# Spreading the first FFN matmul over the attention stages, with its result kept in HBM

## The chip, the cores and the metric

The kernel runs on one core of a Trainium2 chip. The metric is the device time of one execution in microseconds; the time shown is the median of three runs. Engines are named as in the profile: PE is the matmul engine (PEld its weight loads), DVE the vector engine, ACT the scalar engine, POOL GpSimd, and SP the queue that issues every DMA of this kernel. Matmul results go to PSUM, of which the kernel uses eight banks of 128x512 floats.

## The reference

The input x has 2048 rows of 512. Two branches read its layer norm, and the result joins them:

```
xn  = layernorm(x)                                   # [2048, 512]
q, k, v = split(xn @ wqkv)                           # 32 heads of 16
phi(t)  = [softmax(t @ w_phi), softmax(-t @ w_phi)]  # per head, 16 -> 32
kv  = sum over s of phi(k)^T v;   z = sum over s of phi(k)
o   = phi(q) kv / (phi(q) z + 1e-6)
s   = o @ wo
h   = xn @ w1 + b1                                   # [2048, 1792]
g   = silu(mish(h) @ w2)
out = x + s * g
```

Everything is float32. The kernel gets this precision out of the fast matmul format by splitting each operand into a high part hi (rounded) and a low part lo = operand - hi; each product is three matmuls (lo·hi, hi·lo, hi·hi), which is what `mm3` issues.

## The kernel before

The rows are worked in 16 tiles of 128 (t = 0 to 15), in 8 pairs u, and for the FFN in 4 groups g of 512 rows. The 1792 hidden columns make 14 chunks of 128, that is 7 blocks of 256 per group.

The kernel doesn't issue its instructions where they are written. Each call on PE, V (DVE), G (POOL), A (ACT) or Q (SP) is recorded as an `Op` with what it reads and writes. A planner (`Program.simulate`) then plays the program through with a cost for each instruction (`cost`), picks for each engine the ready operation with the earliest due time `late`, and `issue` emits the instructions in the order of the planned starts. The order on PE is not free: it is the order in which the parts are written in the string `ORDER`. An operation recorded by `either` or `copy` may go to one of two engines, which the planner chooses. On the chip each engine then works strictly in the emitted order, and SP's queue too.

The parts in `ORDER`:

- `wk`, `wq`: load the k and q weights and fold w_phi into them (four fp32 matmul groups each), split; `wv`, `wo`: load and split.
- `N t` (`norm`): load x, statistics on DVE, the power -0.5 on POOL (rs), scale, transpose on PE (pt), split into xT, and store xT to HBM (scr) for the FFN.
- `K t` (`k_proj`): 12 matmuls of 128x512, then the double softmax: copy from PSUM (ACT), max and min over 16 (DVE, km), two subtractions (POOL, into ke), exponential (ACT), sums and reciprocal (DVE, ks and kr), scaling (ke), split into kh (ACT) and kl. `Q t` is the same without the split. `V t`: 12 matmuls and a split into vh, vl. `A t` (`kv_acc`): 24 matmuls with 128 columns that add phi(k)^T v into two PSUM banks; v carries a column of ones, which gives z.
- `z` (`sums`): takes kv and z out of PSUM after the last A.
- `D t` (`den`): product with z (ez) and its sums (tz), reciprocal, scaling of phi(q). `T`: transposes of phi(q) (pp) and their split (ph). `U`: 12 matmuls with 256 columns (pn), split into oh, ol. `O t`: 12 matmuls (pw) with wo, stored to HBM (so).
- `P b`, `R b`: load and split block b of w1, w2. `L g`: load group g's xT from scr (tiles fh, fl of the pool; PE's output banks bear the name fh as well).
- `F` (`ffn1`): first FFN matmul of a block, 24 matmuls of 128x512 in two banks, each followed by Mish on ACT, into a tile r that stays in SBUF. `G` (`ffn2`): split of r into ah, al, and 24 matmuls that add into the group's four y banks; the last two blocks of the last group are done together. `E g` (`final`): silu through Tanh, the product, the residual, the store.

Before the change q's projection of a tile stands between the k and v work of the tiles, and of the 28 F blocks six stand ahead of the first G; the other 22 alternate with the G blocks. All SBUF tiles of 4 KB a partition come from one pool of 43 slots, those of 2 KB from one of 11.

Of the kernel before, what the change touches and what calls it, by code (L numbers as in the profile page):

```python
# [28 lines left out]
PEN, HOLD, MARGIN = 8000, 300, 1000  # L29
BACK, COLD = 1500, 0  # L30

SLOTS, S2 = 43, 11
SLACK, AHEAD, LAT = 15000, 40000, 150
ORDER = """
wk K0 wv N2 K1 wq N3 V0 Q0 K2 N4 A0 V1 Q1 K3 N5 A1 V2 Q2 N6 K4 A2 V3 wo K5 Q3 N7 A3 V4 Q4 K6 N8 A4 V5 Q5 K7 N9
A5 V6 Q6 K8 N10 A6 V7 Q7 K9 N11 A7 V8 Q8 K10 N12 A8 V9 Q9 K11 N13 A9 V10 Q10 K12 N14 A10 V11 N15 Q11 b1 P0 K13
A11 V12 L0 P1 Q12 K14 K15 A12 V13 Q13 P2 A13 V14 Q14 A14 V15 Q15 A15 z F0 F1 D0 D1 T0 T1 F2 D2 U0 D3 T2 U1 D4
T3 D5 D6 T4 O1 U2 O0 T5 U3 D7 U4 D9 T6 O3 D8 T7 U5 P3 O2 F3 U6 T8 T9 D11 O4 U7 O5 D10 T10 T11 U8 P4 D12 U9 D13
F4 O7 T12 T13 O8 D14 D15 O6 U10 U11 O9 T14 T15 U12 O11 U13 U14 U15 O13 O10 O12 P5 F5 O15 R0 O14 G0 R1 G1 R2 G2
R3 G3 R4 P6 F6 G4 L1 R5 F7 G5 R6 F8 G6 E0 F9 G7 F10 G8 F11 G9 F12 G10 F13 L2 G11 F14 G12 F15 G13 E1 F16 G14  # L40
F17 G15 F18 G16 F19 G17 F20 G18 L3 F21 G19 F22 G20 E2 F23 G21 F24 G22 F25 G23 F26 F27 G24 G25 G26 E3
"""
# [3 lines left out]
class Op:  # L46
    __slots__ = ("impl", "reads", "writes", "at", "idx", "succ", "ndep", "late", "new", "ready", "start", "eng", "sets", "slack", "open", "soon", "pos", "deps")


class Program:  # L50


    def __init__(self, nc):
        self.eng = {"PE": nc.tensor, "V": nc.vector, "G": nc.gpsimd, "A": nc.scalar, "Q": nc.sync}
        self.ops, self.tag, self.cap, self.pe = [], {}, {}, []
        self.group, self.slack = None, SLACK

# [27 lines left out]
    def add(self, impl, reads, writes, sets=()):  # L85
        o = Op()
        o.impl, o.reads, o.writes, o.idx, o.sets, o.slack = impl, reads, writes, len(self.ops), sets, self.slack
        o.pos = len(self.pe)
        if "PE" in impl:
            self.pe.append(o)  # L90
        self.ops.append(o)
# [64 lines left out]
    def simulate(self, at):  # L156
# [20 lines left out]
        aset = 0  # L177
        dma = 0
        events = [(500, 2, -1)]
# [22 lines left out]
        def go(o, e):  # L202
            nonlocal aset, dma
            dur, calls = o.impl[e]
# [13 lines left out]
            if e == "Q":  # L218
                nb = calls[0][1][0].free_size() * 128 * 4
                dma = max(dma, now + 1100) + nb / 360  # L220
                end = dma + 1000
                heapq.heappush(events, (dma - BACK, 2, -1))
# [93 lines left out]
def block_kernel(ctx: ExitStack, tc: tile.TileContext, x, wqkT, wv, phi, wo, w1, b1, w2, out):  # L316
# [8 lines left out]
    pools = {}  # L325
    for tag, n in (("slot", SLOTS), ("s2", S2), ("sm", 13), ("rq", NT), ("st", 2 * NT)):
        pools[tag] = ctx.enter_context(tc.tile_pool(name=tag, bufs=n))
        prog.cap[tag] = n
# [13 lines left out]
    def slot(shape, name, dtype=F32):  # L342
        return alloc("slot", shape, name, dtype)
# [90 lines left out]

    def load_pairs(src, name):
        r = []
        for i in range(2):
            t = slot([P, 2, D], f"{name}r{i}")
            Q.dma_start(t, src[2 * i * P:2 * (i + 1) * P, :].rearrange("(c p) k -> p c k", p=P))
            hi, lo = split_raw(t, f"{name}{i}")  # L440
            r += [(hi[:, j, :], lo[:, j, :]) for j in range(2)]
        return r

# [63 lines left out]

    def k_proj(t, between=None):
        r = sm([P, 2 * H], f"k{t}r")
        ek[t] = softmax(proj(t, w["k"], "k", between), f"k{t}", r)  # L510
        e = ek[t].rearrange("p h s d -> p (h s d)")
        scale(ek[t], r)
        ek[t] = [slot([P, 2 * D], f"k{n}{t}", F32R) for n in "hl"]
        split(e, *ek[t], either)
# [36 lines left out]

    def tr_q(t):
        u, j = divmod(t, 2)
        if j == 0:
            phT[u] = [[slot([P, 4, 2 * P], f"ph{u}{i}{v}", F32R) for v in range(2)] for i in range(2)]
        e = eq.pop(t).rearrange("p h s d -> p (h s d)")
        cs = slice(j * P, (j + 1) * P)
        for i in range(2):
            pp = bank([P, 4, P], f"pp{t}_{i}")
# [54 lines left out]

    def ffn1(B):
        g, b = divmod(B, NB)
        wh, wl = w1_[b]
        q = slot([P, 2, D], f"r{B}")
        for j2 in range(2):
            f = 2 * b + j2  # L620
            ph = bank([P, D], f"fh{B}_{j2}")
            fs = slice(j2 * P, (j2 + 1) * P)
            with one():
                for k in range(KC):
                    i, kk = divmod(k, 2)
                    mm3(ph, (wh[:, k, fs], wl[:, k, fs]), (fx[g][2 * i][:, kk, :], fx[g][2 * i + 1][:, kk, :]),
                        k == 0, k == KC - 1)
# [49 lines left out]

    def first_k():
        w["k"] = fold(wkT, "wk", 0) + fold(wkT, "wk", 1, lambda: norm(0))

    def weights_v():
        w["v"] = load_pairs(wv, "wv")

    def weights_q():
        t = load_wT(0, "wq", 0) + load_wT(0, "wq", 1)
        w["q"] = fold(t, "wq", 0) + fold(t, "wq", 1)

    def weights_o():
        w["o"] = load_pairs(wo, "wo")

# [26 lines left out]

    def first_proj():
        k_proj(0, lambda: norm(1))

    def att_num(t):
        num(t // 2, t % 2)
# [38 lines left out]
```

## Time and profile before

| | |
|---|---|
| median of three runs | 614.62 us (613.53 to 615.33) |
| the profiled execution's own time | 612.32 us |
| its span, first to last instruction | 610.6 us |
| mean granted TensorE clock | 0.976 |
| busy: PE, DVE, ACT, POOL | 575.0, 357.4, 231.8, 220.7 us |
| DMA | 49.8 MB, mean 82 GB/s |

The page's rows are read so: a busy time is followed by the share of the span and the number of instructions; the slices divide the span into 40 parts of 15.3 us, and a digit is the busy share in tenths. PE's end times are modelled and its matmuls overlap, so PE's busy time is an upper bound of its work. Since everything goes through one helper line, instructions are told apart by their tiles: `al<-r,ah` is the instruction that writes a tile al from r and ah.

### The profile page before, as it was taken

What the parts mean: (1) busy time and instruction counts of PE and PEld (TensorE: products, weight loads), DVE (VectorE), ACT (ScalarE), POOL (GpSimd) and SP (SyncE); (2) the same over time, 40 slices, a digit from 0 to 9 for tenths busy, and PEclk for the clock granted to TensorE, in tenths of its full rate; (3) what the DMA queues carried; (4) which work ended last, traced back from release to release, by engine and by line L of the source; (5) the groups of instructions that cost most, each with busy time, mean ns of one, the idle gap of its engine ahead of it and who ended that gap; (6) DMA issues with size and microseconds to landing.
All of it is one profiled execution on the core that took longest, in us unless ns stands there. A gap on an engine that the chain in (4) does not pass through costs nothing.

```text
span 610.6 us, 7532 instructions
## 1 busy us (share of the span) xinstructions
PE 575.0 (94%) x2998; PEld 484.0 (79%) x2998; DVE 357.4 (59%) x496; ACT 231.8 (38%) x318; POOL 220.7 (36%) x156
## 2 busy tenths in 40 slices
PE   6989999799969978799999999999999999999996
PEld 5868788688758767688888888888888888888885
DVE  6999978888698899999583210801108011081115
ACT  3634444544545442243474122622126221262221
POOL 2787778667666867453131100300003000030000
PEclk9999999989989997799999999999999999999999
DMA  8632212213610002010255700243002430023001
GB/s 283 236 104 79 77 53 74 65 36 101 197 48 0 1 1 70 22 58 27 100 178 185 263 15 0 86 142 119 1 0 89 137 119 0 1 88 137 0 1 69
DMA packets 42211, 49.81 MB, mean 82 GB/s; under 512 B 4160, under 2 KB 27456, under 8 KB 42176
## 3 DMA queue, kind: packets, MB, share of 16 engines
q1 hardware_dynamic: 42176, 49.33, 24.9%
q8 instruction: 23, 0.38, 0.2%
q14 instruction: 12, 0.10, 0.1%
HBM read 32.55 MB, written 16.78 MB: 81 GB/s over the span
## 4 chain that ended last, share of the span: by engine, by line
PE 58%; DVE 21%; POOL 13%; issue 3%; ACT 2%; DMA 1%; SPq 1%; POOLq 0%; DVEq 0%
PE y L300 25%; PE fh L300 21%; PE pw L300 5%; DVE tz L300 3%; PE pn L300 2%; DVE den L300 2%; DVE ph L300 1%; DMA wvr<-wv 1%; DVE x L300 1%; POOL kl L300 1%; PE v L300 1%; PE pp L300 1%; PE kv L300 1%; PE q L300 1%; POOL k2e L300 1%
## 5 line engine op out<-in xcount | busy, mean ns | idle before, releaser
L300 DVE TENSOR_TENSOR al<-r,ah 128x1024 fp32r<-128x1024 f32 x21 | 25.7, 1224 | 141.8 <-ACT ah L300 141.7
L300 ACT ACTIVATE r<-fh,b1t 128x512 f32<-128x512 f32 x56 | 38.1, 689 | 165.3 <-PE fh L300 165.3
L300 POOL TENSOR_TENSOR al<-r,ah 128x1024 fp32r<-128x1024 f32 x7 | 17.0, 2426 | 211.1 <-ACT ah L300 211.1
L300 PE MATMUL k<-wkh,xT 128*128 128x512 f32 x128 | 42.5, 393 | 0.7 <-DVE xT L300 0.7
L300 PE MATMUL q<-wqh,xT 128*128 128x512 f32 x128 | 42.1, 390 | 0.0
L300 PE MATMUL kv<-kh,vl 128*65 128x128 f32 x128 | 26.7, 240 | 12.3 <-DVE vl L300 11.6
L300 PEld LDWEIGHTS kv<-kh,vl 128*65 128x65 f32 x128 | 18.9, 147 | 14.6 <-DVE vl L300 14.4
L300 PE MATMUL pn<-ph,kvh 128*128 128x256 f32 x128 | 24.8, 293 | 5.8 <-DVE ph L300 5.8
L300 ACT ACTIVATE ah<-r 128x1024 fp32r<-128x1024 f32 x28 | 29.6, 1059 | 0.7
L300 PEld LDWEIGHTS k<-wkh,xT 128*128 128x128 f32 x128 | 24.0, 188 | 5.8 <-DVE xT L300 0.9
L300 PEld LDWEIGHTS q<-wqh,xT 128*128 128x128 f32 x128 | 24.0, 188 | 5.0
L300 PE MATMUL kv<-kl,vh 128*65 128x128 f32 x128 | 26.0, 235 | 0.7 <-DVE kl L300 0.7
L300 PE MATMUL kv<-kh,vh 128*65 128x128 f32 x128 | 25.9, 234 | 0.0
L300 PEld LDWEIGHTS pn<-ph,kvh 128*128 128x128 f32 x128 | 20.7, 199 | 6.5 <-DVE ph L300 6.3
L300 PE MATMUL v<-wv0h,xT 128*128 128x512 f32 x64 | 25.3, 437 | 0.0
L300 PE MATMUL k<-wkl,xT 128*128 128x512 f32 x64 | 24.9, 390 | 0.0
L300 PE MATMUL q<-wql,xT 128*128 128x512 f32 x64 | 24.9, 389 | 0.0
L300 PE MATMUL v<-wv1h,xT 128*128 128x512 f32 x64 | 22.7, 395 | 0.0
L300 DVE TENSOR_TENSOR ph<-pp,ph 128x512 fp32r<-128x512 f32 x32 | 20.6, 679 | 3.4 <-ACT ph L300 3.4
L300 DVE TENSOR_TENSOR sr<-yc,sr 128x512 f32<-128x512 f32 x12 | 20.4, 1699 | 0.5
L300 DVE COPY yc<-y 128x512 f32<-128x512 f32 x6 | 4.1, 685 | 27.6 <-PE y L300 27.6
L300 PEld LDWEIGHTS kv<-kl,vh 128*65 128x65 f32 x128 | 18.9, 148 | 1.3 <-DVE kl L300 0.9
(573 smaller groups left out, 1814.3 us busy)
## 6 DMA issues: line engine op xcount, KB each, us to landing
scr<-xT SPq DMA_DIRECT2D x16, 512.0 KB, 3.8
x<-x SPq DMA_DIRECT2D x16, 256.0 KB, 4.0
fh<-scr SPq DMA_DIRECT2D x8, 512.0 KB, 4.9
fl<-scr SPq DMA_DIRECT2D x8, 512.0 KB, 5.3
so<-so SPq DMA_DIRECT2D x16, 256.0 KB, 2.2
sr<-so SPq DMA_DIRECT2D x15, 256.0 KB, 5.2
xx<-x SPq DMA_DIRECT2D x15, 256.0 KB, 4.6
out<-xx SPq DMA_DIRECT2D x15, 256.0 KB, 2.0
```

The source lines that it names most:

```text
L300: getattr(e, m)(*a, **k)
```

## The change

F is cut in 56 pieces: one output chunk of 128 columns for a group of 512 rows, 12 matmuls of 128x512. Its bank is copied to a tile h by ACT or DVE, without bias or Mish, and stored to an HBM tile hd. G loads the two halves of its block from hd into r, applies Mish in place on ACT, and goes on as before. `ORDER` places 55 of the 56 pieces ahead of the first G, among K, V, A and Q, D, T, U, O; 15 of the 16 O tiles stand ahead of the first G as well, where before all 16 did. Loading w1 (`P`) and the groups (`L`) moves forward with the pieces. Most Q parts stand after the last A (seven tiles ahead of it, nine behind), and q reads its x from scr again instead of keeping xT. The halves of wk, wv, wq and wo are parts of their own, and T and U are cut by halves of the heads instead of tiles.

The planner changes in three ways. It keeps a time `port` until which the pair of VectorE and GpSimd is taken: an operation that `locks` names (any on G; on V those with two SBUF operands beside the output, or a wide tensor_scalar or copy, none reading PSUM) starts its duration only from then. DMA is planned with 250 instead of 360 bytes per ns. A PE operation no longer depends on an earlier PE operation, since PE works in order anyway.

```diff
-BACK, COLD = 1500, 0
+BACK, COLD, DRATE = 1500, 0, 250
...
+            if "PE" in o.impl:
+                dep = {d for d in dep if "PE" not in ops[d].impl}
...
+            if e in o.lock:
+                dur += max(0, port - now)
+                port = now + dur
...
-                dma = max(dma, now + 1100) + nb / 360
+                dma = max(dma, now + 1100) + nb / DRATE
...
+def locks(e, m, a):
+
+    if e == "G":
+        return True
+    aps = [v for v in a if isinstance(v, bass.AP)]
+    if e != "V" or any(v.space == "PSUM" for v in aps):
+        return False
+    return aps[0].free_size() > 1 if m in ("tensor_scalar", "tensor_copy") else len(aps) > 2
...
     def q_proj(t):
+        xT[t] = slot([P, 2, KC, P], f"xq{t}", F32R)
+        Q.dma_start(f32(xT[t]), scr[t // 4][:, :, :, t % 4, :])
...
-    def ffn1(B):
-        g, b = divmod(B, NB)
+    def ffn1(n):
+        g, f = divmod(n, FC)
+        b, j2 = divmod(f, 2)
         wh, wl = w1_[b]
...
-            A.activation(q[:, j2, :], ph, AF.Mish, bias=b1t[:, f:f + 1])
-        acts[B] = q
+        h = s2(f"h{n}")
+        copy(h, ph)
+        Q.dma_start(hd[g * NB + b][:, j2, :], h)
...
     def ffn2(B):
...
-            q = acts.pop(b)
...
+            q = slot([P, 2, D], f"r{b}")
+            Q.dma_start(q, hd[b])
+            for j2 in range(2):
+                f = 2 * (b % NB) + j2
+                A.activation(q[:, j2, :], q[:, j2, :], AF.Mish, bias=b1t[:, f:f + 1])
+            ah, al = split_raw(q, f"a{b}")
```

Of `ORDER`, the first lines stand so before and after:

```diff
-wk K0 wv N2 K1 wq N3 V0 Q0 K2 N4 A0 V1 Q1 K3 N5 A1 V2 Q2 N6 K4 A2 V3 wo K5 Q3 N7 A3 V4 Q4 K6 N8 A4 V5 Q5 K7 N9
+N0 N1 wv0 wk0 wk1 K1 N2 K0 wv1 V0 N4 N5 P0 N3 K3 A0 V1 K2 P2 L0 A1 V2 N6 K4 K5 P1 F2 F0 A2 V3 K6 P5 N12 A3 V4 wq0 N8
+N9 F3 P6 P3 P4 A4 V5 N7 F10 wq1 F12 N10 K7 F1 A5 V6 F6 K8 A6 V7 L1 N11 F4 F8 K10 F18 F19 F5 F14 A7 F13 V8 K9 F15 F16
```

PE in the first stage, around the projection k of tile 5 (names are tile, number, then the buffer's number). Before, q of tile 3 follows it:

```order
L300 MATMUL k5_266<-wkl1_136,xT5_235 128x512
L300 MATMUL k5_266<-wkh1_135,xT5_235 128x512
L300 MATMUL q3_274<-wqh0_181,xT3_193 128x512
L300 MATMUL q3_274<-wql0_182,xT3_193 128x512
L300 MATMUL q3_274<-wqh0_181,xT3_193 128x512 x2
```

After, the first FFN piece (chunk 2 of group 0) stands there, ahead of the kv sums of tile 2:

```order
L307 MATMUL k5_241<-wkl1_151,xT5_190 128x512
L307 MATMUL k5_241<-wkh1_150,xT5_190 128x512
L307 MATMUL fh2_252<-fh00_221,w11l_250 128x512
L307 MATMUL fh2_252<-fl00_222,w11h_249 128x512
L307 MATMUL fh2_252<-fh00_221,w11h_249 128x512
```

The piece needs tiles 0 to 3 normalised, stored and loaded again as a group (fh00, fl00), and w1's block 1 split (w11h, w11l). On SP's queue the same stretch before holds loads of x and stores of xT only:

```order
L300 DMA scr1_107<-xT4_214 1024x1x128
L300 DMA x9_321<-x 128x512
L300 DMA scr1_107<-xT5_235 1024x1x128
L300 DMA x10_342<-x 128x512
L300 DMA scr1_107<-xT6_248 1024x1x128
L300 DMA x11_363<-x 128x512
```

After, group 0, w1's blocks and the first pieces' stores stand in it:

```order
L307 DMA fh00_221<-scr0_106 128x1024
L307 DMA fl00_222<-scr0_106 128x1024
L307 DMA fh01_223<-scr0_106 128x1024
L307 DMA fl01_224<-scr0_106 128x1024
L307 DMA x9_287<-x 128x512
L307 DMA wqT00_276<-wqkT 128x4x256
L307 DMA x7_305<-x 128x512
L307 DMA w1r5_266<-w1 128x4x256
L307 DMA scr1_107<-xT6_230 1024x1x128
L307 DMA hd01_251<-h2_253 128x512
```

The loads of x for tile 8 and on, and of w1's next blocks, have moved behind the group's loads, and a store of h may stand ahead of a load. The third place is ACT in the second FFN stage. Before, it takes Mish of the blocks from PE's banks (fh):

```order
L300 ACTIVATE r12_811<-fh12_0_812,b1t_83 128x512
L300 ACTIVATE r12_811<-fh12_1_813,b1t_83 128x512
L300 ACTIVATE ah12_828<-r12_811 128x1024
L300 ACTIVATE r13_816<-fh13_0_817,b1t_83 128x512
L300 ACTIVATE r13_816<-fh13_1_818,b1t_83 128x512
L300 ACTIVATE ah13_833<-r13_816 128x1024
```

After, at the start of that stage, Mish reads the tile r that a DMA has brought back, between the last attention tiles (oh) and w2's splits:

```order
L307 ACT_TABLE_LOAD
L307 ACTIVATE r0_885<-r0_885,b1t_83 128x512 x2
L307 ACTIVATE a0h_886<-r0_885 128x1024
L307 ACTIVATE oh7_863<-pn7_0_865 128x512
L307 ACTIVATE r7_898<-r7_898,b1t_83 128x512 x2
L307 ACTIVATE oh7_863<-pn7_1_869 128x512
L307 ACTIVATE a7h_899<-r7_898 128x1024
```

Mish no longer waits for PE there, but for the load of r.

More of the change, by code (lines that the diff above doesn't have):

```diff
@@ L34 @@
 ORDER = """
-wk K0 wv N2 K1 wq N3 V0 Q0 K2 N4 A0 V1 Q1 K3 N5 A1 V2 Q2 N6 K4 A2 V3 wo K5 Q3 N7 A3 V4 Q4 K6 N8 A4 V5 Q5 K7 N9
[L36 to L41, printed above, removed]
+N0 N1 wv0 wk0 wk1 K1 N2 K0 wv1 V0 N4 N5 P0 N3 K3 A0 V1 K2 P2 L0 A1 V2 N6 K4 K5 P1 F2 F0 A2 V3 K6 P5 N12 A3 V4 wq0 N8
+N9 F3 P6 P3 P4 A4 V5 N7 F10 wq1 F12 N10 K7 F1 A5 V6 F6 K8 A6 V7 L1 N11 F4 F8 K10 F18 F19 F5 F14 A7 F13 V8 K9 F15 F16
+N13 A8 V9 F24 F11 F25 A9 V10 Q9 K11 F22 A10 V11 L2 F30 K12 F7 N14 F9 N15 K13 A11 V12 F20 Q4 K15 K14 Q0 A12 F21 V13 Q1
+A13 V14 F17 Q2 Q6 b1 A14 V15 Q5 A15 F23 z Q3 D0 F26 F27 D1 Q8 F28 F34 L3 T1 D3 T0 F32 D2 Q7 F31 Q12 F29 U0 U1 wo0 wo1
+T3 D6 F35 T2 F38 U2 U3 F36 F39 D5 F33 O0 D4 O1 F37 D7 D8 F42 F46 F43 F44 F40 Q10 F41 T6 T5 T4 Q11 U4 U5 T7 D9 T8 T9
+D12 Q13 Q14 D14 U8 U9 F50 U6 D11 U7 O2 F48 F49 F45 O3 F51 R2 O5 Q15 D10 T11 O8 D15 F54 F52 D13 T10 T12 O7 U10 O6 T13
+U11 R6 O9 F47 T15 T14 U12 U13 R0 O10 U14 R4 U15 O4 F53 O11 R3 O15 O13 O12 G0 R1 R5 G7 G8 G1 G2 G3 G4 G9 G10 G11 G5 G6
+O14 G12 E0 G13 E1 G14 G15 F55 G16 G17 G18 G19 G20 E2 G21 G22 G23 G24 G25 G26 E3
 """
@@ L46 @@
 class Op:
-    __slots__ = ("impl", "reads", "writes", "at", "idx", "succ", "ndep", "late", "new", "ready", "start", "eng", "sets", "slack", "open", "soon", "pos", "deps")
+    __slots__ = ("impl", "reads", "writes", "at", "idx", "succ", "ndep", "late", "new", "ready", "start", "eng", "sets", "slack", "open", "soon", "pos", "deps", "lock", "part")
 class Program:
@@ L55, in __init__ @@
         self.ops, self.tag, self.cap, self.pe = [], {}, {}, []
-        self.group, self.slack = None, SLACK
+        self.group, self.slack, self.part = None, SLACK, None
     @staticmethod
@@ L87, in add @@
         o.impl, o.reads, o.writes, o.idx, o.sets, o.slack = impl, reads, writes, len(self.ops), sets, self.slack
-        o.pos = len(self.pe)
+        o.pos, o.part = len(self.pe), self.part
+        o.lock = {e for e, (_, calls) in impl.items() if any(locks(e, m, a) for m, a, k in calls)}
         if "PE" in impl:
@@ L177, in simulate @@
         aset = 0
-        dma = 0
+        dma = port = 0
         events = [(500, 2, -1)]
@@ L202, in go @@
         def go(o, e):
-            nonlocal aset, dma
+            nonlocal aset, dma, port
             dur, calls = o.impl[e]
@@ L325, in block_kernel @@
     pools = {}
-    for tag, n in (("slot", SLOTS), ("s2", S2), ("sm", 13), ("rq", NT), ("st", 2 * NT)):
+    for tag, n in (("slot", SLOTS), ("s2", S2), ("sm", 13), ("rq", 5), ("st", 2 * NT)):
         pools[tag] = ctx.enter_context(tc.tile_pool(name=tag, bufs=n))
@@ L414, in load_wT, with fold @@
         return ts
-    def fold(wT, name, i, between=None):
+    def fold(wT, name, i):
         hi = slot([P, 2, D], f"{name}h{i}", F32R)
@@ L424, in fold @@
             split(ps, hi[:, j, :], lo[:, j, :])
-            if between and j == 0:
-                between()
         return [(hi[:, j, :], lo[:, j, :]) for j in range(2)]
@@ L433, in split_raw, with load_pair @@
         return hi, lo
[L435 to L442, printed above, removed]
+    def load_pair(src, name, i):
+        t = slot([P, 2, D], f"{name}r{i}")
+        Q.dma_start(t, src[2 * i * P:2 * (i + 1) * P, :].rearrange("(c p) k -> p c k", p=P))
+        hi, lo = split_raw(t, f"{name}{i}")
+        return [(hi[:, j, :], lo[:, j, :]) for j in range(2)]
     scr = [dram.tile([P, 2, KC, 4, P], F32, name=f"scr{g}") for g in range(NG)]
@@ L470, in norm, with proj @@
         Q.dma_start(scr[t // 4][:, :, :, t % 4, :], f32(w))
-    def proj(t, w, name, between=None):
+    def proj(t, w, name):
         ps = bank([P, D], f"{name}{t}")
@@ L477, in proj @@
                     mm3(ps, (xT[t][:, 0, k, :], xT[t][:, 1, k, :]), w[k], k == 0, k == KC - 1)
-            if between and i == 0:
-                between()
         return ps
@@ L506, in block_kernel, with k_proj @@
     ek, eq, rq, phT, oT = {}, {}, {}, {}, {}
-    def k_proj(t, between=None):
+    def k_proj(t):
         r = sm([P, 2 * H], f"k{t}r")
[L510 to L514, printed above, removed]
+        e = softmax(proj(t, w["k"], "k"), f"k{t}", r)
+        scale(e, r)
+        ek[t] = split_raw(e.rearrange("p h s d -> p (h s d)"), f"k{t}")
     def q_proj(t):
+        xT[t] = slot([P, 2, KC, P], f"xq{t}", F32R)
+        Q.dma_start(f32(xT[t]), scr[t // 4][:, :, :, t % 4, :])
         rq[t] = alloc("rq", [P, 2 * H], f"q{t}r")
@@ L550, in den, with tr_q @@
         scale(eq[t], r)
[L552 to L559, printed above, removed]
+    def tr_q(n):
+        u, i = divmod(n, 2)
+        phT[n] = [slot([P, 4, 2 * P], f"ph{u}{i}{v}", F32R) for v in range(2)]
+        for j in range(2):
+            e = eq[2 * u + j].rearrange("p h s d -> p (h s d)")
+            cs = slice(j * P, (j + 1) * P)
+            pp = bank([P, 4, P], f"pp{2 * u + j}_{i}")
             with one():
@@ L562, in tr_q, with num @@
                     PE.transpose(pp[:, c, :], e[:, (4 * i + c) * P:(4 * i + c + 1) * P], ident)
-            split(pp, phT[u][i][0][:, :, cs], phT[u][i][1][:, :, cs])
-    def num(u, i):
-        ph = phT[u][i]
+            split(pp, phT[n][0][:, :, cs], phT[n][1][:, :, cs])
+    def num(n):
+        u, i = divmod(n, 2)
+        ph = phT.pop(n)
         if i == 0:
@@ L604, in prep2 @@
         w2_[b] = split_raw(t, f"w2{b}")
+    hd = {}
     def load_g(g):
@@ L613, in load_g @@
                 fx[g].append(t)
-    def ffn1(B):
-        g, b = divmod(B, NB)
+    def ffn1(n):
+        g, f = divmod(n, FC)
+        b, j2 = divmod(f, 2)
         wh, wl = w1_[b]
[L618 to L627, printed above, removed]
-            A.activation(q[:, j2, :], ph, AF.Mish, bias=b1t[:, f:f + 1])
-        acts[B] = q
+        if j2 == 0:
+            hd[g * NB + b] = dram.tile([P, 2, D], F32, name=f"hd{g}{b}")
+        ph = bank([P, D], f"fh{n}")
+        fs = slice(j2 * P, (j2 + 1) * P)
+        with one():
+            for k in range(KC):
+                i, kk = divmod(k, 2)
+                mm3(ph, (wh[:, k, fs], wl[:, k, fs]), (fx[g][2 * i][:, kk, :], fx[g][2 * i + 1][:, kk, :]),
+                    k == 0, k == KC - 1)
+        h = s2(f"h{n}")
+        copy(h, ph)
+        Q.dma_start(hd[g * NB + b][:, j2, :], h)
     def ffn2(B):
@@ L633, in ffn2 @@
         for b in (B, B + 1) if B == NBT - 2 else (B,):
-            q = acts.pop(b)
-            ah = slot([P, 2, D], f"ah{b}", F32R)
-            al = slot([P, 2, D], f"al{b}", F32R)
-            split(q, ah, al, either)
+            q = slot([P, 2, D], f"r{b}")
[4 more added lines that the diff above has]
+            ah, al = split_raw(q, f"a{b}")
             todo.append((b % NB, ah, al, *w2_[b % NB]))
@@ L676, in block_kernel, with weights_k, weights_v, weights_q @@
     w = {}
[L678 to L689, printed above, removed]
+    def weights_k(i):
+        w.setdefault("k", []).extend(fold(wkT, "wk", i))
+    def weights_v(i):
+        w.setdefault("v", []).extend(load_pair(wv, "wv", i))
+    def weights_q(i):
+        wqT.extend(load_wT(0, "wq", i))
+        w.setdefault("q", []).extend(fold(wqT, "wq", i))
+    def weights_o(i):
+        w.setdefault("o", []).extend(load_pair(wo, "wo", i))
     def bias():
@@ L716, in sums @@
         w["z"], w["kv"] = zt, (kvh, kvl)
[L718 to L722, printed above, removed]
+    wqT = []
     wkT = load_wT(D, "wk", 0, 2) + load_wT(D, "wk", 1)
-    parts = {"wk": first_k, "wv": weights_v, "wq": weights_q, "wo": weights_o, "b1": bias, "z": sums, "K0": first_proj,
-             "N": norm, "K": k_proj, "V": v_proj, "A": kv_acc, "Q": q_proj, "D": den, "T": tr_q, "U": att_num,
+    parts = {"b1": bias, "z": sums,
+             "wk": weights_k, "wv": weights_v, "wq": weights_q, "wo": weights_o, "N": norm, "K": k_proj, "V": v_proj, "A": kv_acc, "Q": q_proj, "D": den, "T": tr_q, "U": num,
              "O": att_out, "L": load_g, "P": prep1, "R": prep2, "F": ffn1, "G": ffn2, "E": final}
     for c in ORDER.split():
+        prog.part = c
         if c in parts:
@@ L731, in block_kernel @@
         else:
-            parts[c[0]](int(c[1:]))
+            n = c.rstrip("0123456789")
+            parts[n](int(c[len(n):]))
     prog.issue()
```

## Prediction

> **What bounds the kernel now.** I read the page first: busy shares, slices, the chain's shares.
>
> ```profile
> span 610.6 us, 7532 instructions
> PE 575.0 (94%) x2998; PEld 484.0 (79%) x2998; DVE 357.4 (59%) x496; ACT 231.8 (38%) x318; POOL 220.7 (36%) x156
> PE   6989999799969978799999999999999999999996
> DVE  6999978888698899999583210801108011081115
> PEclk9999999989989997799999999999999999999999
> PE 58%; DVE 21%; POOL 13%; issue 3%; ACT 2%; DMA 1%; SPq 1%; POOLq 0%; DVEq 0%
> ```
>
> PE is busy 94%, but its holes, and DVE's nines, lie in the first 22 slices. Next the windows, one row a stretch: start:end, length, busy time of PE, PEld, DVE, ACT and POOL, clock, DMA share, GB/s.
>
> ```profile
> 0.00:71.50 71.50, 63.68 (x382) 53.79 (x383) 62.66 (x107) 33.47 (x46) 45.60 (x50) 1.00 0.47 155
> 71.50:200.00 128.50, 117.57 (x711) 98.12 (x710) 107.19 (x147) 60.43 (x81) 92.43 (x70) 0.95 0.26 74
> 200.00:332.60 132.60, 121.10 (x666) 104.91 (x666) 110.13 (x152) 56.56 (x90) 63.91 (x28) 0.95 0.20 67
> 295.00:333.00 38.00, 38.00 (x211) 33.16 (x210) 19.67 (x21) 20.34 (x29) 7.41 (x4) 1.00 0.48 158
> 332.60:602.40 269.80, 269.80 (x1220) 224.61 (x1220) 72.83 (x82) 79.96 (x100) 18.78 (x10) 1.00 0.21 72
> 175.00:180.00 5.00, 0.38 (x2) 0.00 (x0) 3.70 (x5) 2.60 (x3) 5.00 (x4) 0.89 0.31 92
> 180.00:185.00 5.00, 4.54 (x29) 4.15 (x30) 4.97 (x8) 2.02 (x3) 2.59 (x3) 0.50 0.05 17
> 245.00:250.00 5.00, 0.98 (x4) 0.98 (x5) 4.93 (x6) 0.09 (x1) 2.02 (x1) 0.71 0.00 0
> 250.00:255.00 5.00, 5.00 (x24) 4.68 (x23) 4.16 (x5) 1.79 (x3) 1.42 (x1) 0.60 0.00 0
> 160.00:165.00 5.00, 5.00 (x24) 4.14 (x23) 1.56 (x3) 1.54 (x2) 4.84 (x5) 1.00 0.97 260
> ```
>
> Busy PE time overstates work: matmuls overlap, and slow-clock ones count long. The chain in order of time (start, length, count) gives true prices where PE alone carries it.
>
> ```profile
> 190.01 1.45 PE kv L300 x24
> 194.28 2.72 PE q L300 x12
> 290.43 1.75 PE pp L300 x16
> 305.01 1.44 PE pn L300 x12
> 354.33 5.44 PE fh L300 x24
> 583.12 19.25 PE y L300 x96
> ```
>
> So a 128x512 matmul costs 5.44/24 = 0.227 us, a kv one 0.060, a pn one 0.120, a transpose 0.109. Counted over the program: 48 projections, 56 FFN pieces and 16 output tiles of 2.72 us; 28 second-FFN blocks of 5.44 (5.51 in the last group); 16 kv tiles of 1.45, 16 pn of 1.44; 192 transposes, the folds and z some 29. PE's work is 555.3 us of the 610.6.
>
> From the first y to the end PE needs 272.7 and has no hole; after its last matmul the last tile's ACT, DVE and output take 5.3. The other 282.6 take 332.6, so all else, 50 us, is lost ahead of the first y. There DVE is busy 62.66 + 107.19 + 110.13 = 280 of 332.6. Up to 71.5 us, where PE's work adds up to 60, the loss is 11.5; later 38.5.
>
> The loss has a second part. After the empty five microseconds at 175 and 245 the granted clock of the next five is 0.50 and 0.60.
> The Trainium skill (TensorE: Matmul & The Clock Gate, Part 1: The HAM clock gate) says that about 3.4 us of idleness halves PE's clock until it has again been busy as long; by that rule, the trace agrees, and fillers that break such holes save their slow microseconds too. My sum has those inside the 38.5.
>
> **The change, part by part.**
>
> Moving first-FFN pieces. Before, 44 of the 56 stand after the first y; now one, with one output tile. PE's work behind the first y becomes 272.7 - 44 x 2.72 + 2 x 2.72 = 158.4, ahead of it 396.9. No matmul is added or dropped: floor 396.9 + 158.4 + 5.3 = 560.6.
>
> Work of the other engines ahead of the first y. These rows price it (the last four columns: mean ns, idle before, releaser).
>
> ```profile
> L300 ACT ACTIVATE r<-fh,b1t 128x512 f32<-128x512 f32 x56 | 38.1, 689 | 165.3 <-PE fh L300 165.3
> L300 ACT ACTIVATE so<-pw 128x512 f32<-128x512 f32 x14 | 8.4, 598 | 28.0 <-PE pw L300 28.0
> L300 DVE TENSOR_TENSOR al<-r,ah 128x1024 fp32r<-128x1024 f32 x21 | 25.7, 1224 | 141.8 <-ACT ah L300 141.7
> L300 DVE TENSOR_TENSOR kl<-k7e,kh 128x1024 fp32r<-128x1024 f32 x1 | 2.1, 2074 | 0.0
> L300 POOL TENSOR_TENSOR al<-r,ah 128x1024 fp32r<-128x1024 f32 x7 | 17.0, 2426 | 211.1 <-ACT ah L300 211.1
> L300 DVE TENSOR_TENSOR xT<-pt,xT 128x512 fp32r<-128x512 f32 x16 | 10.8, 676 | 0.0
> L300 DVE TENSOR_REDUCE tz<-ez 128x64 f32<-128x1024 f32 x16 | 19.1, 1204 | 0.8 <-POOL ez L300 0.8
> 26.72 1.94 POOL L300 TENSOR_TENSOR k0e<-k0e,k0r 128x1024 f32<-128x1024 f32 x1 [2.29 <-DVE k0r L300]
> 17.67 1.05 POOL L300 TENSOR_TENSOR k0e<-k0p,k0m 128x512 f32<-128x512 f32 x1
> 16.39 1.28 DVE L300 TENSOR_REDUCE k0m<-k0p 128x32 f32<-128x512 f32 x2 [0.70 <-ACT k0p L300]
> 14.41 0.51 DVE L300 TENSOR_SCALAR x<-x,mv,rs 128x512 f32<-128x512 f32 x1
> L300 DVE BATCH_NORM_STATS2 st<-x 128x6 f32<-128x512 f32 x16 | 10.9, 678 | 2.9 <-DMA x<-x 2.9
> L300 POOL TENSOR_TENSOR rs<-rs,mhalf 128x1 f32<-128x1 f32 x16 | 8.7, 548 | 11.7 <-DVE rs L300 11.5
> L300 ACT ACT_TABLE_LOAD x9 | 11.5, 1283 | 0.9 <-PEq L753 0.8
> ```
>
> By the order of both kernels at undisturbed prices (1024-wide subtraction on DVE 1.22 or POOL 2.4, reduction 0.66 or 1.20, subtraction from PSUM 0.68, halves of e 1.05, scaling 1.94), ahead of the first y DVE has 261 us before and 264 now, POOL 186 and 200, ACT 161 and 195. Against PE this was 261 to 283, a tie that each chain's waits broke; now it is 264 to 397, two thirds. 56 copies of fh (53 on ACT, 3 on DVE) at 0.60 add 34 us to ACT, two table loads 2.6; ACT, at some 270 of 585, has room. Mish stays, now from SBUF.
>
> The first stretch, up to the fourth FFN piece: eleven N, seven K, six V, five A, seven w1 blocks' splits, both halves of wv and wk, one of wq. PE has 61.1. DVE: twelve statistics with their small steps 12 x 1.0, eleven x and xT 11 x 1.20, seven softmaxes 7 x (2 x 0.66 + 1.20 + 0.53), nine wide operations at 1.22, eleven subtractions from PSUM at 0.68, together 66. POOL: 14 halves at 1.05, five scalings at 1.94, nine wide at 2.4, twelve rs at 0.55, with the set-up 55. Were POOL's 55 and DVE's wide operations and x (17.6) never to overlap, that would be 72.6. The pair kl at 2074 and al at 1224, same shape, shows the disturbance: +0.85 us with POOL busy. So this stretch stays bound by DVE and POOL; before, PE's same 60 took 71.5 with DVE busy 62.66. Bounds of the loss: 8 (DVE's 66 and a small start) and 20 (72.6 and a start of 8). I take 14, near the row's 11.5 with three w1 blocks more.
> The Trainium skill (SBUF — State Buffer, SBUF: two separate sides) calls the pair of ports that DVE and POOL share an exclusive lock for a whole instruction, which speaks against seven splits ahead of the fourth piece; the trace agrees in direction with 2074 to 1224. By it the loss would be 72.6 - 61.1 plus a start, about 16; without it about 8.
>
> The middle, 335.8 us of PE's work with DVE at 198, 59%. Bounds of the loss: 0, as in the row 295 to 333, where DVE had 19.67 of 38 (52%) and PE no hole; and 38.5, if every chain's wait stays. It is nearest to the first, but some 60 us of PE's order there (q beside transposes and den) still have DVE at 80 to 93%. At such a load (71.5 to 200, DVE 107.19 of 128.5) PE did 109 of work, a loss of 15%; 15% of 60 is 9. I take 10, which includes the start of G.
>
> The last stage: per G block of 5.44 two Mish (0.69), one ah and one al must come, some 2.4 on ACT and 1.2 on DVE; E adds to that. Blocks 12 to 17 are the tightest: by count 33 of ACT on 38 of PE. I cost it at nothing, covered by blocks prepared some four ahead; without that lead about 5 us.
>
> Transfers. Rows of issues (KB, median us to landing):
>
> ```profile
> scr<-xT SPq DMA_DIRECT2D x16, 512.0 KB, 3.8
> fh<-scr SPq DMA_DIRECT2D x8, 512.0 KB, 4.9
> so<-so SPq DMA_DIRECT2D x16, 256.0 KB, 2.2
> q1 hardware_dynamic: 42176, 49.33, 24.9%
> ```
>
> hd adds 56 stores of 256 KB and 28 loads of 512 KB; q's x comes back in 16 loads of 512 KB: 49 becomes 87 MB, 100 issues more on SP's queue. On average 149 GB/s, where the row at 160 shows 260. A load there waits behind a store whose h is late, and the next FFN piece or Mish behind it; their lead (x for q, r) hides it, else it is inside the middle's bounds. Behind the first y stand 23.9 MB in 158.4 us, 151 GB/s: also hidden. Moving q's projections, transposes and sums past the kv sums changes no count; it takes wq and wo off the first loads, where three w1 blocks take their place.
>
> Sum: 560.6 + 14 + 10 = 584.6 of span. The profiled execution took 612.32, 1.7 over its span, and the median shown is 2.3 above that: 588.6, say 588.
>
> **The rivals.**
>
> 1. Half the middle's waits stay: PE obeys its order, and a piece is no filler if it stands behind the late kv or ph instead of before it. For it: the chain is 34% DVE and POOL. Against: 59% load. 560.6 + 14 + 24 + 4 = 603.
>
> 2. It fills nothing: all 38.5 stay, since the pieces wait for their own w1 splits and scr loads. 560.6 + 14 + 38.5 + 4 = 617, or about 615, no change (a change under 0.3%, 2 us, can't be told from none). Against: with 114 us more of PE's work beside the same chains they would have to grow as long again.
>
> 3. Slower: the last stage is left without first-FFN matmuls to cover r's loads, and becomes bound by transfers. Its place is G; its rate must be 151 GB/s to cost nothing, and from 23.9/(158.4 + 26) = 130 downwards the whole gain is gone. At 110 GB/s it takes 217, 59 more: 647. For it: a load's 4.9 us to landing is nearly a block's 5.44, and before this stage needed only 72. Against: 260 at 160 us, and loads run several at once.
>
> **How the numbers follow.** Forecast 0.62, rival 1 0.22, rival 2 0.06, rival 3 0.10. The forecast's own range is 580 to 597: below by the first stretch at 8 and the middle near 7, above by 20 and 12. Rival 1 reaches to 606; up to there lies 0.8, leaving rivals 2 and 3. Faster 0.84 (first two), same 0.05, slower 0.11.
>
> **What would show it.** Right: PE without a hole from about 80 us, first y near 421, DVE's nines only in the first four slices, clock near 1.00, the chain over 80% PE. First stretch wrong if the fourth piece ends far from 75. Rival 1: waits of PE for kl, vl, ph between 100 and 400. Rival 3: ACT r or ah waiting for DMA r<-hd, and y rows slower than 5.44 a block.

## The result and the profile after

The changed kernel takes 587.21 us (median of four runs, 586.99 to 587.57), the kernel before 614.83 in the same comparison: a ratio of 0.9555, 95% interval 0.9538 to 0.9571. The forecast was 588 in 580 to 606. The page of the changed kernel, with its slices and chain:

```profile
span 585.3 us, 7901 instructions
PE 566.2 (97%) x2998; PEld 477.5 (82%) x2998; DVE 355.6 (61%) x486; ACT 265.0 (45%) x371; POOL 246.4 (42%) x171
PE   5799999999999999999997999999999999999996
DVE  6999975425145675986374899755532306855705
PEclk9999999999999999999997999999999999999999
PE 91%; DVE 5%; POOL 2%; DMA 1%; ACT 1%; issue 0%; POOLq 0%; SPq 0%
```

Apart from the last slice PE has two places below nine, the first two slices and slice 22 (307 to 322 us), and the only slice with a slow clock is slice 22. The chain is PE for 91% of the span, where it was 58% before. The windows and the chain by time (a few pieces):

```profile
0.00:29.00 29.00, 18.57 (x97) 15.57 (x98) 23.30 (x48) 14.95 (x21) 14.92 (x28) 0.96 0.79 255
29.00:75.00 46.00, 45.89 (x303) 39.12 (x302) 43.13 (x57) 25.24 (x34) 43.86 (x27) 0.99 0.75 233
80.00:200.00 120.00, 120.00 (x666) 100.68 (x665) 53.30 (x78) 40.66 (x58) 35.91 (x29) 1.00 0.40 128
309.00:322.00 13.00, 9.59 (x31) 7.35 (x30) 5.51 (x14) 1.20 (x2) 4.93 (x3) 0.74 0.44 141
421.00:580.00 159.00, 159.00 (x742) 133.31 (x740) 72.17 (x73) 79.78 (x102) 32.27 (x19) 1.00 0.44 151
...
8.63 4.05 PE wkf L307 x32
76.19 2.77 PE fh L307 x12
421.84 65.28 PE y L307 x288
```

From 29 us on PE has work, and the first y starts at 421.84, where 421 was forecast. Ahead of it lie 421.84 - 396.9 = 24.9 us of loss, half of the 50 of before.

PE's waits are few now (total, times, longest):

```profile
PE pt L307 <- DVE rs L307: 5.9, 1, 5.9
PE q L307 <- DMA xq<-scr: 3.4, 1, 3.4
PE pt L307 <- DVE x L307: 3.0, 3, 1.5
PE k L307 <- DVE xT L307: 1.5, 1, 1.5
```

### The profile page after: what moved, and what is told of

The parts are those of the page before. It is cut to its first block, busy times and chain, and to the rows that moved or that the text cites. A ratio compares the mean times of both kernels' runs of the same rounds, so it can differ in the third digit from the quotient of the medians.

```text
span 585.3 us, 7901 instructions
## 1 busy us (share of the span) xinstructions
PE 566.2 (97%) x2998; PEld 477.5 (82%) x2998; DVE 355.6 (61%) x486; ACT 265.0 (45%) x371; POOL 246.4 (42%) x171
## 4 chain that ended last, share of the span: by engine, by line
PE 91%; DVE 5%; POOL 2%; DMA 1%; ACT 1%; issue 0%; POOLq 0%; SPq 0%
PE y L307 26%; PE fh L307 23%; PE q L307 8%; PE pw L307 7%; PE v L307 7%; PE k L307 6%; PE kv L307 4%; PE pn L307 4%; PE pp L307 2%; PE pt L307 1%; DVE den L307 1%; DVE tz L307 1%; DMA xq<-scr 1%; PE wkf L307 1%; PE wqf L307 1%; DVE x L307 0%
## 5 line engine op out<-in xcount | busy, mean ns | idle before, releaser
L307 ACT ACTIVATE h<-fh 128x512 f32<-128x512 f32 x53 | 31.8, 600 | 91.0 <-PE fh L307 83.5
L307 POOL TENSOR_TENSOR xx<-u,xx 128x512 f32<-128x512 f32 (+1 forms) x11 | 15.8, 1448 | 96.3 <-DVE u L307 96.3
L307 ACT ACTIVATE r<-r,b1t 128x512 f32<-128x512 f32 x56 | 37.7, 716 | 27.9 <-DMA r<-hd 27.8
L307 PE MATMUL q<-wqh,xq 128*128 128x512 f32 x128 | 44.0, 408 | 3.5 <-DMA xq<-scr 3.4
L307 PEld LDWEIGHTS q<-wqh,xq 128*128 128x128 f32 x128 | 25.1, 196 | 9.6 <-issue 3.8
L307 PEld LDWEIGHTS k<-wkh,xT 128*128 128x128 f32 x128 | 24.7, 193 | 6.9 <-DVE xT L307 1.8
L307 PE MATMUL q<-wql,xq 128*128 128x512 f32 x64 | 25.9, 404 | 0.0
L307 DVE TENSOR_TENSOR vl<-v,vh 128x512 fp32r<-128x512 f32 x16 | 11.0, 685 | 22.2 <-ACT vh L307 22.2
L307 PE MATMUL v<-wv1h,xT 128*128 128x512 f32 x64 | 22.6, 393 | 0.0
L307 DVE TENSOR_REDUCE tz<-ez 128x64 f32<-128x1024 f32 x16 | 19.2, 1204 | 1.3 <-POOL ez L307 1.2
L307 ACT ACTIVATE ph<-pp 128x512 fp32r<-128x512 f32 x32 | 17.6, 603 | 4.9 <-PE pp L307 4.9
L307 PE MATMUL pn<-ph,kvl 128*128 128x256 f32 x64 | 18.2, 285 | 0.0
```

What stands on the lines that cost most here:

```text
L307: getattr(e, m)(*a, **k)
```

## The experiments

The theory that the prediction stood on: PE work (the FFN pieces) beside the attention chains takes up the 38 us that their waits cost. The rivals are the other two parts of the change, the planner's model and q's new place, and for single steps those named below. Times are medians; each ratio is to the kernel before, run on the same chip.

| run | what | us | ratio (95% interval) | loss ahead of the first y, us |
|---|---|---|---|---|
| e12 | the changed kernel again | 587.03 | 0.9569 (0.9549 to 0.9589) | 24.5 |
| e1 | new order, planner as before | 598.27 | 0.976 (0.9734 to 0.9785) | 35.3 |
| e3 | order of before, new planner | 593.18 | 0.968 (0.9654 to 0.9705) | 34.4 |
| e3a | order of before, port alone | 597.90 | 0.974 (0.9718 to 0.9762) | 35.8 |
| e3c | order of before, PE-PE dependences out | 607.69 | 0.9907 (0.9883 to 0.9931) | 43.9 |
| e10 | half of the pieces spread | 619.29 | 1.0102 (1.0067 to 1.0137) | 57.7 |
| e2 | no piece spread | 648.13 | 1.0572 (1.0538 to 1.0607) | 86.1 |
| e5 | r loaded twice | 588.12 | 0.9587 (0.9568 to 0.9607) | 23.9 |
| e7 | w1's low part not subtracted | 587.40 | 0.9574 (0.9557 to 0.9591) | 24.7 |
| e8 | N3, K3 earlier | 591.07 | 0.9637 (0.9605 to 0.967) | 26.7 |
| e6 | F41 and Q10 exchanged | 585.25 | 0.9529 (0.9506 to 0.9552) | 22.6 |
| e11 | that, and K2 earlier | 583.47 | 0.951 (0.9486 to 0.9533) | 22.3 |

The last column is the span of the profiled execution less the floor of 560.6 us (PE's 555.3 and the 5.3 at the end). A profiled execution need not be a typical one: that of e3 took 596.72, 3.5 more than its median, so that e3's loss by the median would be some 31. In none of these runs does PE have a hole above 0.1 us between the first y and its last matmul.

### The planner's model, in either order

In the changed program the three changes of the planner are undone:

```diff
-BACK, COLD, DRATE = 1500, 0, 250
+BACK, COLD, DRATE = 1500, 0, 360
-            if "PE" in o.impl:
-                dep = {d for d in dep if "PE" not in ops[d].impl}
-            if e in o.lock:
-                dur += max(0, port - now)
-                port = now + dur
```

> The changed program, parts in the new order, with the planner's three changes undone (no port, 360 bytes per ns, PE operations depend on earlier PE operations). PE's order stays as it is; only which of DVE, POOL and ACT takes an operation, and when, can differ. Theory (the gain is PE work standing beside the attention chains, not the planner's model): 587 to 595 us, PE holes of a few us more. Rival (the model of the port made the gain): 600 us or more.

It took 598.27: worse than the theory's range, better than the rival's. The new order alone is worth 15 us, and the planner the other 11. Where the 11 lie is read from PE's longest wait, at the start, the only two kinds of wait behind the fourth piece (ph and vl), and the chain by time:

```profile
PE pt L302 <- DVE x L302: 7.1, 1, 7.1
PE pn L302 <- DVE ph L302: 2.9, 2, 2.4
PE kv L302 <- DVE vl L302: 1.7, 1, 1.7
...
87.89 2.77 PE fh L302 x12
432.50 65.28 PE y L302 x288
```

The fourth piece ends at 87.89 + 2.77 = 90.66 here, at 78.96 in the changed kernel; from there to the first y it is 341.8 us against 342.9. In the new order the planner's 11 us thus lie wholly ahead of the fourth piece, and behind it the pieces hold PE busy without the planner's help. Which of its three changes counts at the start was not tried in this order.

The kernel before gets the same three changes, and keeps its `ORDER`, F, G and q.

> The kernel before with the new planner alone (port, 250 bytes per ns, no PE-PE dependence), its order of parts unchanged. Theory: within 5 us of before, 608 to 616, the loss ahead of the first y still above 40 us, since PE's work there still equals DVE's. Rival (the port model itself removes the waits): 600 or less.

It took 593.18. The theory's 608 to 616 fell, and its loss of more than 40 us with it: 20 of the 27 us come without moving a single piece. The views of PE's waits, before and with the new planner:

```profile
PE kv L300 <- DVE vl L300: 11.6, 6, 5.1
PE pn L300 <- DVE ph L300: 5.8, 2, 4.5
PE pp L300 <- DVE ol L300: 3.6, 1, 3.6
```

```profile
PE pp L306 <- POOL q4e L306: 2.8, 1, 2.8
PE pp L306 <- DVE q7e L306: 2.2, 1, 2.2
PE pp L306 <- POOL q1e L306: 1.9, 1, 1.9
PE kv L306 <- DVE kl L306: 1.7, 1, 1.7
```

The waits for vl, ph and ol are gone and none of those left in the middle is longer than 2.8 us; busy times and clock of the stretches quoted in the prediction are now:

```profile
0.00:71.50 71.50, 63.74 (x366) 54.73 (x367) 58.18 (x95) 33.67 (x46) 46.01 (x49) 0.98 0.48 155
71.50:200.00 128.50, 125.64 (x763) 104.82 (x762) 115.73 (x164) 67.65 (x86) 105.61 (x79) 0.97 0.25 74
200.00:332.60 132.60, 124.20 (x701) 107.52 (x700) 96.48 (x140) 57.53 (x91) 74.08 (x34) 1.00 0.29 96
PE 570.7 (96%) x2998; PEld 481.4 (81%) x2998; DVE 347.8 (58%) x466; ACT 237.5 (40%) x322; POOL 269.9 (45%) x184
```

The first three rows are windows (the last of them reaches past the first y, at 317 here), the fourth is of its page. By 71.5 us PE has begun 366 matmuls, where it was 382 before, so it is some 4 us behind there; the gain all lies in the middle, where the loss is some 19 instead of 38.5. The planner has moved work from DVE to POOL (357.4 and 220.7 us before), although POOL takes longer for the same operation (2426 ns against 1224 for al in the prediction's rows). Which of the three changes did it was tried on the kernel before, one at a time:

```diff
+            if e in o.lock:
+                dur += max(0, port - now)
+                port = now + dur
```

> The kernel before with the port's time in the planner alone (360 bytes per ns and the PE-PE dependences stay). The planner's three changes together gave 593 where under 616 was expected from the theory of fillers alone. Theory (it is the port: planned starts come nearer to the chip's, DVE and POOL get their work in an order without surprises, and PE's long holes with their slow clock go): 592 to 597. Rival (it is the PE-PE dependence, which made the plan's PE late): 606 or more.

```diff
+            if "PE" in o.impl:
+                dep = {d for d in dep if "PE" not in ops[d].impl}
```

> The kernel before with the PE-PE dependences taken out of the planner alone (no port, 360 bytes per ns). Theory of the port: 608 to 616. Rival (the dependences): 600 or less.

The port alone gives 597.90, just above the range that its theory gave, the dependences alone 607.69, just under theirs. The port is the larger part (2.6% of 3.2), the dependences 0.9%. If the two add, they make 3.5%, and nothing is left for the slower DMA of the plan; that was not run by itself. That the port works through the choice of engine is argued from the busy times, not shown: order and choice changed together.

### How much the pieces do

The parts F0 to F54 are taken out of the attention stages and stand in a row ahead of G0, with L1 to L3 just ahead of their groups:

```diff
-... N6 K4 K5 P1 F2 F0 A2 V3 K6 P5 N12 A3 V4 ...
+... N6 K4 K5 P1 A2 V3 K6 P5 N12 A3 V4 ...
...
+... O13 O10 O12 F1 F2 F3 F4 ... F54 G0 ...
```

> The changed program with the 55 FFN pieces gathered in one run between the last output tile and the first G; q still behind the kv sums, h still through HBM, the new planner. Theory: without pieces the stages of K, V, A and of Q, D, T, U, O are again bound by DVE and POOL (DVE 264 us of undisturbed work ahead of the first y, PE 247 there without the pieces), the pieces then run bare: about 165 + 145 + 150 + 164 = 620 us, between 610 and 632. Rival (the gain is q's move or the planner): under 600.

Only groups 0 and 1 stay spread, groups 2 and 3 stand two ahead of each G from G0 on (the G blocks here one group after the other, since two groups' y banks leave none of the kernel's eight for a piece):

```diff
-... T5 T4 F41 Q11 ... O12 G0 R1 R5 G7 ...
+... T5 T4 Q11 ... O12 R1 R5 O14 F28 F29 G0 F30 F31 G1 ...
```

> The changed program with the pieces of groups 0 and 1 spread as before, those of groups 2 and 3 (28) moved behind the first G, two ahead of each G. The stage of K, V, A keeps its fillers, that of D, T, U, O (behind the kv sums at about 235 us) keeps one. Theory: the first stage stays near 235, the second is bound by DVE's some 140 us there, then 28 pieces and the G blocks run dense: 235 + 145 + 76 + 153 + 5 = 614, between 605 and 622. Rival (half the fillers are enough, since PE lost little per us of DVE): 590 to 596.

The direction was the theory's, the size of the first was not: 648 instead of 610 to 632. The half took 619.29, within its 605 to 622. Windows of the one without spreading:

```profile
0.00:200.00 200.00, 170.44 (x1032) 142.89 (x1033) 161.56 (x237) 88.39 (x117) 134.29 (x108) 0.92 0.44 132
200.00:318.00 118.00, 92.46 (x495) 80.53 (x493) 103.91 (x154) 46.76 (x75) 82.53 (x47) 0.83 0.22 70
318.00:482.00 164.00, 164.00 (x733) 136.12 (x732) 16.09 (x17) 54.53 (x82) 2.40 (x1) 1.00 0.52 175
285.00:290.00 5.00, 1.07 (x4) 0.71 (x4) 4.97 (x6) 0.00 (x0) 4.55 (x3) 0.50 0.00 0
```

Up to 318 us DVE is busy for 83% and the clock is 0.92 and 0.83, with stretches like that at 285 where PE has next to nothing and runs at half clock; then the pieces run bare, with DVE at 10%. Of the 86 us of loss, PE stands idle for 55.1 by the first two rows; most of the other 31 is slow clock (PE is busy at half clock for 45.8 us, which costs some 23), and my estimate (whose terms add to 624, not 620) had left that out. With q behind the kv sums and without pieces the order is far worse than the one before (86 us of loss against 50). With the same planner the old order loses 34, the new one without pieces 86, the new one with them 25: the rest of the change (q's place, the order around it, the halves, h through HBM) costs 52, and the pieces bring 61. The 61 hold for this order alone, which was made for the pieces; both together bring some 10 over the old order with the same planner, and by the medians, 593.18 and 587.03, only 6.

### The first stretch

The low half of w1 is written as zeros by ACT:

```diff
-        w1_[b] = split_raw(t, f"w1{b}")
+        A.activation(hi, t, AF.Copy)
+        A.activation(lo, t, AF.Copy, scale=0.0)
+        w1_[b] = hi, lo
```

> The changed kernel, in which the low half of w1 is written as zeros by ACT instead of being subtracted on DVE or POOL (the FFN's products lose their low part of w1). It takes seven wide operations, 15 us of DVE or POOL work, out of the stretch up to the fourth piece, and puts 7 us on ACT. Theory of the prediction (that stretch as a whole is bound by DVE and POOL): the fourth piece ends 4 to 8 us earlier, 579 to 583 us. Rival (the loss is the start's own chain, x, statistics, xT, over by 29 us, and the splits are hidden behind PE from then on): 585.5 to 588.

587.40, no change. The windows of this run, which answer to those of the changed kernel above:

```profile
0.00:29.00 29.00, 18.67 (x97) 15.65 (x98) 23.35 (x48) 15.51 (x22) 14.97 (x28) 0.96 0.77 255
29.00:75.00 46.00, 45.89 (x303) 39.17 (x302) 39.53 (x65) 30.65 (x39) 32.36 (x25) 0.99 0.74 225
```

POOL is 11.5 us less busy from 29 to 75 us, and PE's 45.89 stays the same to the hundredth. Nearly all of the first stretch's loss lies ahead of 29 us.

Then the order at the start, where PE waits for x and xT of tiles 4, 5 and 3:

```diff
-... K0 wv1 V0 N4 N5 P0 N3 K3 A0 ...
+... K0 wv1 V0 N3 K3 N4 N5 P0 A0 ...
```

> The changed kernel with N3 and K3 moved ahead of N4, N5 and P0, so that the statistics and splits of tiles 4 and 5 no longer stand ahead of the x and xT of tile 3, for which PE waits three times (4.0 us in all) between 22 and 28 us. Theory (DVE's order there, not its total, makes these holes): 1.5 to 3 us faster, 584 to 586. Rival (DVE is simply full from 10 to 30 us): within 1 us of 587, the holes only move.

591.07, slower by about 4 us and outside both: a miss. Of its six runs three took 589.0 and three 593 to 594. In the profiled one, of the first kind, the holes moved to k (1.92 us for xT) and behind it to the first kv sums, whose k0h and k0l came later; what the other three lost more is not shown.

### The hole at 314 us

The chain of the changed kernel into that hole (start, length):

```profile
294.68 2.41 POOL ez L307
...
304.15 1.83 DVE den L307
...
306.39 1.97 DVE q4r L307
308.35 1.14 DVE tz L307
...
309.55 4.59 DMA xq<-scr
...
314.27 5.46 PE q L307 x12
```

The load of x for q is issued only when the tz of an earlier tile has ended: the chain's step is a tile that comes free, not a transfer queue. Twelve matmuls then take 5.46 instead of 2.72, on the half clock behind the hole. That the clock falls there is not certain: in e12, the same program, it does not.

```profile
PE q L307 <- DMA xq<-scr: 3.6, 1, 3.6
...
235.00:240.00 5.00, 5.00 (x19) 3.29 (x18) 4.64 (x4) 1.44 (x2) 2.37 (x1) 0.66 0.79 231
315.00:320.00 5.00, 3.16 (x14) 2.63 (x15) 0.40 (x1) 0.07 (x1) 2.19 (x1) 1.00 0.91 306
```

Behind a hole of 3.6 us the clock stays at 1.00 and the twelve matmuls take 3.01. A slow clock stands at 237 us instead, just behind z, where PE has no hole, and q takes 4.47 there, 2.97 in the changed kernel's profile. The spans are 585.1 and 585.3. The exchange:

```diff
-... F40 Q10 F41 T6 ...
+... F40 F41 Q10 T6 ...
```

> The changed kernel with the parts F41 and Q10 exchanged, so that one more FFN piece (2.72 us of PE) stands ahead of the projection that waits 3.41 us for the load of its x at 314 us; about as much is lost to the slow clock behind that hole. Theory (hole plus slow clock cost some 6 us, and a filler ahead takes both): 581 to 584. Rival (the load waits for a free slot, and the slots shift with the exchange, so the hole only moves): 586 to 589.

```profile
309.00:316.00 7.00, 7.00 (x32) 5.79 (x32) 6.97 (x14) 1.20 (x2) 5.23 (x3) 1.00 0.24 66
```

The hole is gone (7.00 of 7.00, clock 1.00) and the time is 585.25, between the two ranges. That is less than the 3 to 6 us expected: the span fell by 2.1, because in the profiled run the start was 1.2 us longer and some 3 us came back between 235 and 332 us (the slow clock at z, as in e12, and two waits of 0.6). By intervals, 0.9506 to 0.9552 against 0.9538 to 0.9571, they still touch, so this gain is not certain. With K2 moved ahead of the transposes as well:

```diff
-... K0 wv1 V0 N4 N5 P0 N3 K3 A0 V1 K2 P2 ...
+... K0 wv1 V0 K2 N4 N5 P0 N3 K3 A0 V1 P2 ...
```

> The changed kernel with F41 ahead of Q10, and the projection K2, whose x is ready early, moved from behind V1 to behind V0, ahead of the transposes of tiles 4, 5 and 3 that wait for DVE between 22 and 28 us. If those holes (4.0 us, and the slow clock behind them) are a matter of what PE has ready there: 578 to 582 us. If they are a matter of DVE's total up to 30 us: 584 to 587, the holes move behind K2.

> The changed kernel itself once more, on the same chip as the two-swap version, for a comparison within half a per cent: 586 to 588.

583.47 and 587.03 on the same chip, with intervals that don't touch (0.9486 to 0.9533, 0.9549 to 0.9589): the version with both exchanges is faster than the changed kernel, and has the lowest median of all, though its interval overlaps with that of e6. It lies between the two ranges. What K2 does in it is not shown to be a gain; the holes at 22 to 28 us shrink, one of 2.7 us opens at the second kv sum, which waits for vl, and the fourth piece ends at 81.56, later than the 80.20 of e6:

```profile
PE kv L307 <- DVE vl L307: 2.7, 1, 2.7
PE pt L307 <- DVE x L307: 1.5, 2, 0.9
```

### The last stage's transfers

```diff
+            q2 = slot([P, 2, D], f"rr{b}")
+            Q.dma_start(q2, hd[b])
             Q.dma_start(q, hd[b])
```

> The changed kernel, with each block's 512 KB of hd loaded a second time into a slot of its own that nothing reads: 14.7 MB more, 10.5 of them behind the first y, so 34 MB in 158 us, 217 GB/s instead of 151. Theory (the last stage is bound by PE, transfers are hidden): 587 to 591 us. Rival (the last stage stands close to the transfers' bound): 600 or more.

```profile
424.00:580.00 156.00, 155.10 (x724) 129.91 (x722) 67.18 (x71) 83.37 (x106) 40.82 (x22) 1.00 0.68 241
q1 hardware_dynamic: 74944, 101.77, 51.6%
```

588.12: with 241 GB/s instead of 151 through the last stage PE still has 155.1 of 156, and the missing 0.9 is behind its last matmul. Transfers have room there; rival 3 of the prediction is far off.

## Why the prediction was right, and where it was not

**Floor, 560.6.** Right: the y rows behind 421.84 have no hole, and their 65.28 us for 288 matmuls are 0.227 each, as before.

**The first stretch, 14.** Size right, step wrong. I put it down to DVE and POOL being full up to the fourth piece. That piece ended at 78.96, later than 75 (3.0 of this because that sum, unlike the floor, counted the folds at half: wk alone takes 4.05). But from 29 us on PE was held by nothing, with DVE at 43.13 and POOL at 43.86 of 46, and taking 11.5 us off POOL changed nothing (e7). The loss is nearly all the start: 5.9 us until the first rs, 4.0 in three waits for x and xT, and the rest short overlaps and a clock of 0.83 for a while. From 10 to 30 us DVE is busy for 19.1, so load may count there, but how large the loss is depends on how the work is planned: with the same parts on PE and the planner as before the stretch loses 26.6 instead of 14.9 (e1). Two of the sums are also 1 us too high: DVE's terms add to 65.0 and not to 66, its wide operations and x, at the rows shown, to 16.6 and not to 17.6. Of the two figures set against each other there, 16 by the port's rule and 8 without, the total came nearer to the first, but for another reason: e7 took the splits away, and the loss stayed.

**The middle, 10.** Right in size, and in mechanism: from the end of the fourth piece to the first y 342.9 us passed on 332.8 of PE's work, 10.1 of loss, and without the new planner it is 9.0 (e1). In the profiled execution some 6.5 lie in one hole and its slow clock (the lead that was to hide the load of q's x failed this once), 2 at z, where the four fp32 matmuls pz take 1.9 us for which no price was set apart. The row that I took as nearest, PE without a hole at 52% of DVE, held for 80 to 200 us (DVE 53.30 of 120).

**The planner: the step that failed.** Its changes got no term of their own. I read the order that it makes, but priced only the moved work, and ascribed the whole 27 us to the pieces. The runs give it 20 us with the old order and 11 with the new; new order without it 15. These don't add up to 27, since the gains overlap, and not in the same place. In the old order the planner alone takes 19 of the middle's 38.5, so the sentence that fails is that DVE's 261 against PE's 283 is a tie broken by each chain's waits, as though 38 us of loss came with the tie: with the same parts in the same order half of it goes. In the new order the pieces take nearly 30 of the 38.5 without it, but the start loses 26.6 where it lost 11.5 before, hence the 15; the planner's 11 lie there, in the term of 14 that I had put down to load.

**Luck.** The span was 585.3 where the sum said 584.6, and of the 2.3 us added from the profiled execution to the median 0.2 came about. That 588 lies so near to 587.2 is in part luck, since the reason for the 14 fails for most of its stretch; that the pieces fill the middle is not.

**Rivals.** The time of rival 1 came about in e1 (598), for the order without the new planner, but not its reason: the middle lost only 9.0 there. Rival 2's reason, that the pieces wait for their own inputs, came about nowhere: no piece is among PE's waits in the changed kernel or e1. Rival 3 fell with e5. One of its two signs did show in the changed kernel, and cost nothing, since the y rows kept their 0.227 a matmul:

```profile
ACT r L307 <- DMA r<-hd: 27.8, 9, 7.8
```

**What would show it.** The clock (0.989), the chain (91%) and the first y were as said, and PE's work from 80 us on too, but for the hole of 3.4 us at 311. DVE's nines stand in slices 2 to 5, and return at slices 17, 24 and 25, where q stands beside z, den and transposes, and almost no hole of PE falls into them.

## What to carry over

When a planner's model of the engines changes, run the old order with the new model before crediting the order; here the model alone gave three quarters of the gain, and the order alone more than half. Then ask where each gain lies: a part that is worth nothing in the middle can still be worth 11 us at the start. Work that fills an engine's holes is worth the holes and, where the clock falls behind them, the slow matmuls too. Which holes those are can't be read from their length here: 3.4 us was followed by half clock, 3.6 in another execution of the same program was not, and at 26 us waits of at most 1.5 were (0.66 from 25 to 30 us). A stretch in which a side engine is 90% busy need not hold the main one up: take that work out once and see.

## What was not expected of the hardware

Small operations of DVE are lengthened beside POOL's by more microseconds than the wide ones in the prediction's rows (2074 against 1224 ns). In the changed kernel q4r, 64 columns, took 1.97 us beside a POOL multiplication, where its like take 0.22, and den, 32 columns, goes from 0.18 to 2.27 (start and length in the first two rows, of the timeline; the others list a tile's instructions):

```profile
305.87 2.40 POOL L307 TENSOR_TENSOR ez<-q8e,zb 128x1024 f32<-128x1024 f32 x1
306.39 1.97 DVE L307 TENSOR_TENSOR q4r<-q4r,den 128x64 f32<-128x64 f32 x1
...
L307 DVE SCALAR_TENSOR_TENSOR den<-tz x16: 177/192/2266, 244.7 to 380.9; 128x32 f32<-128x32 f32 x16
L307 DVE TENSOR_TENSOR q5r<-q5r,den x1: 224/224/224, 301.3 to 301.3; 128x64 f32<-128x64 f32 x1
```

The durations are minimum, median and maximum in ns. The Trainium skill (SBUF — State Buffer, SBUF: two separate sides) says that the pair of ports is held for a whole instruction and the other engine waits; these rows agree: q4r ends at 308.36, with POOL's ez at 308.27. So it is with all eleven operations on tz, den and q's r that took over 0.9 us: each ends within 0.1 us after an operation of POOL. One tile's tz, den and q4r, between 302.7 and 308.4 us, took 0.94, 1.90 and 1.97 us, where their like take some 0.2 each, so a plan with 0.2 for each has what waits for them 4 us too early.
